# Where the first transposing loads stand in the load queue, and where the first block of x is turned

## The chip, the cores and the metric

The kernel runs on one core of one Trainium2 chip. The metric is the device time of one execution in microseconds (us); a time given for a kernel is the median of its runs. A profile shows one further execution on the same kind of core.

## The reference

Two independent attention blocks, A and B, of the same size (S = 2048 rows, D = 640, 32 heads of 20), whose outputs stand side by side in the result:

```python
B, S, D = 1, 2048, 640            # bf16; wqkv (640, 1920), wo (640, 640)

def _A_ref(x, wqkv, wo):          # causal softmax attention in a window of 256 keys
    H = 32; Dh = D // H; W = 256
    qkv = (x @ wqkv).reshape(B, S, 3, H, Dh).transpose(2, 0, 3, 1, 4)
    q, k, v = qkv[0], qkv[1], qkv[2]
    scores = jnp.einsum("bhqd,bhkd->bhqk", q, k) * (Dh ** -0.5)
    mask = (idx[:, None] - idx[None, :] >= 0) & (idx[:, None] - idx[None, :] < W)
    p = softmax(jnp.where(mask, scores, -1e9))
    o = jnp.einsum("bhqk,bhkd->bhqd", p, v)
    return o.transpose(0, 2, 1, 3).reshape(B, S, D) @ wo

def _B_ref(x, wqkv, wo):          # linear attention over all rows
    ...
    pq, pk = phi(q), phi(k)       # phi(t) = where(t > 0, t + 1, exp(t)) + 1e-6
    kv = jnp.einsum("bhsd,bhse->bhde", pk, v)
    z = jnp.einsum("bhsd->bhd", pk)
    o = jnp.einsum("bhqd,bhde->bhqe", pq, kv) / (jnp.einsum("bhqd,bhd->bhq", pq, z)[..., None] + 1e-6)
    return o.transpose(0, 2, 1, 3).reshape(B, S, D) @ wo

return jnp.concatenate([_A_ref(A_x, A_wqkv, A_wo), _B_ref(B_x, B_wqkv, B_wo)], axis=-1)
```

## The kernel before

The rows are worked on in four blocks of 512 (SB). D is cut into five tiles of 128 (KT), so a projection is a chain of five matmuls that add up in one bank of PSUM; the banks named "dense" are four and are used in turn. An evacuation (`evac`) copies a finished bank to SBUF; it goes to ACT or to DVE after a running count of what each has been given. Every engine works through its instructions in the order in which the program lists them, and waits where an operand isn't there yet. All loads and stores are issued on SP's queue, in program order as well.

A matmul needs x with its columns on the partitions, that is, transposed. There are two ways to that. `load_x` and `load_part` let the DMA transpose while it loads (`dma_start_transpose`, in the profile DMA_TRANSPOSE): a whole block of x at line 162, a quarter of a block at line 938. `load_x_first` does it for the first block of A's x alone: two plain loads bring 256 rows each (line 172, into a tile that the profile calls phi), and `transposes(i)` has PE turn them in blocks of 128 x 128 (line 178, ten for each half), after which DVE copies one 128-row block to xA and ACT the other (lines 184 and 186).

At the start SP issues, in this order: x's first half; v's weights wA in two parts (line 948: kt 0 and 1, 320 KB, then kt 2 to 4, 480 KB; K0 = 2 is the cut); x's second half; the raw weights of q and of k (line 335, 800 KB each, into tiles that the profile calls qpad and kpad); the transposing load of A's second block, xA[1]; B's key weights wB (line 156, 800 KB); the transposing load of B's first block, xB[0].

PE runs 28 dummy products (line 197) while the first load is on its way, then turns x's first half, runs three more dummies, and projects v of the first block. v is made by 128 rows and half of the heads at a time, eight chains of five products of 320 columns (line 412). The first four chains are made by `v_abreast`: the first two products of all four, then the other three of each. Then x's second half is turned, and `v_proj` makes the other four chains one after the other. Among them stand the calls of `regroup`, in which DVE, ACT and POOL rearrange the raw weights of q (behind the sixth chain) and of k (behind the eighth) into wqk, in which the heads are spaced by 32 columns (lines 350, 353 and 356).

Then come three chains of q and two of k (line 277, five products of 512 columns each), and with them the main loop starts: tiles of scores (line 762), their exponentials on ACT (line 780), masks on POOL (line 794), products with v (line 821). Between the tiles, `take` fills PE with the chains of a `plan`, sorted by due times written out by hand: the rest of q and k of the first block, q of the second block (the first use of xA[1]), B's keys (`b_keys(0)`, the first use of xB[0] and wB), and so on to the output projections. The plan holds DMA issues too: `keep_x(0)` (line 927) writes xB[0] to DRAM for later; the writes and reads at lines 375 and 384 move the part of q and k of the first block that belongs to heads of the groups from 5 on to other partitions by way of DRAM.

The order at the start, as the program lists it:

```python
    raw = [load_raw(i) for i in range(2)]
    xA[1] = load_x("A", 1)
    load_w("B", B_wqkv, 1, nc.sync)
    xB[0] = load_x("B", 0)
    ...
    v_abreast(xA[0], v_tok[0], by_tokens[0:4], K0)
    transposes(1)
    a_v0 = v_proj(xA[0], v_tok[0], by_tokens[4:])
    run(banks(a_v0, 2))
    regroup(0, raw[0], dve_copy, in_turn(act_copy, pool_copy))
    run(a_v0)
    regroup(1, raw[1], in_turn(dve_copy, act_copy), in_turn(act_copy, pool_copy))
```

Of the kernel before, what the change touches and what calls it, by code (L numbers as in the profile page):

```python
# [92 lines left out]
def kernel(  # L93
# [10 lines left out]
    nc = tc.nc  # L104
    _, S, D = A_x.shape
    KT = D // P
# [46 lines left out]
    def load_w(n, src, i, eng):  # L153
        wv = src.rearrange("(kt p) n -> p kt n", p=P)
        cols = slice(i * D, (i + 1) * D)
        eng.dma_start(out=w_sb[n][:, :, cols], in_=wv[:, :, cols])

    xsrc = {"A": A_x[0], "B": B_x[0]}

    def load_x(n, s):  # L160
        t = xp.tile([P, KT, SB], BF16, name=f"x{n}")
        nc.sync.dma_start_transpose(out=t[:], in_=xsrc[n][s * SB : (s + 1) * SB, :])
        return t

# [25 lines left out]
    def warm_up(wait):  # L190

        z = op.tile([P, TPS, D], BF16, name="osb")
        nc.vector.memset(z[:, 0, 0:P], 0.0)
        ps = dps.tile([P, SB], F32, name="dense")
        for n in wait:
            for _ in range(n):
                nc.tensor.matmul(
                    ps[:, 0:P], lhsT=z[:, 0, 0:P], rhs=z[:, 0, 0:P], start=True, stop=True
                )
            yield  # L200
# [27 lines left out]
    def flush(before=None):  # L228

        while later and (before is None or later[0][0] <= before):  # L230
            later.pop(0)[1]()
# [9 lines left out]
    def settle(all=True):  # L241
        while posts and (all or posts[0][0] <= begun[0]):
            posts.pop(0)[1]()
# [12 lines left out]
    def evac(dst, src, n=SB, to=None):  # L256

        if to is None:
            to = "A" if load["A"] < load["D"] + AHEAD else "D"
        load[to] += n + COPY  # L260
        if to == "A":
            nc.scalar.activation(out=dst, in_=src, func=ACT.Copy)
        else:
            nc.vector.tensor_copy(out=dst, in_=src)

    def bank(wide=False):
        flush(begun[0] - 2)
        begun[0] += 1
        settle(False)
        if wide:  # L270
            return dps.tile([P, 2 * SB], BF16, name="dense")
        return dps.tile([P, SB], F32, name="dense")
# [32 lines left out]
    def banks(g, n):  # L305

        for _ in range(n):
            for c in g:
                yield c
                if isinstance(c, End):  # L310
                    break

    xA, xB = {}, {}
    q_pad, k_pad, v_tok = {}, {}, {}
# [7 lines left out]
    for c in range(KT):  # L322
        m = EXTRA * c
        while m < EXTRA * (c + 1):
            n = min(EXTRA * (c + 1) - m, DH - m % DH)
# [3 lines left out]
    def load_raw(i):  # L329

        pl, name = ((qp, "qpad"), (kp, "kpad"))[i]
        t = pl.tile([P, NG, SB], BF16, name=name)
        raw = t.rearrange("p g q -> p (g q)")[:, 0 : KT * D].rearrange("p (k n) -> p k n", n=D)
        wv = A_wqkv.rearrange("(kt p) n -> p kt n", p=P)
        nc.sync.dma_start(out=raw, in_=wv[:, :, i * D : (i + 1) * D])
        return raw

    def regroup(i, src, heads, extras):

        def four(g):  # L340
            return src[:, :, 4 * DH * g : 4 * DH * (g + 1)].rearrange("p k (j d) -> p k j d", d=DH)

        for c in range(KT):
            dst = wqk[:, i, :, c * P : (c + 1) * P].rearrange("p k (j e) -> p k j e", e=32)
            heads(dst[:, :, :, 0:DH], four(c))
            for _, row, g, d, n in [piece for piece in pieces if piece[0] == c]:
                extras(dst[:, :, :, row : row + n], four(g)[:, :, :, d : d + n])
# [10 lines left out]
    def in_turn(*fns):  # L358
        n = [0]

        def copy(dst, src):
            n[0] += 1
            fns[n[0] % len(fns)](dst, src)

        return copy
# [43 lines left out]
    by_tokens = [(tb, i) for tb in range(TPS) for i in range(2)]  # L409

    def v_product(ps, xt, tb, i, kt):
        nc.tensor.matmul(  # L412
            ps[:, 0 : hh * DH],
            lhsT=xt[:, kt, tb * P : (tb + 1) * P],
            rhs=w_sb["A"][:, kt, i * hh * DH : (i + 1) * hh * DH],
            start=(kt == 0),
            stop=(kt == KT - 1),
        )

    def v_rows(ps, dst, tb, i):  # L420
        evac(
            dst[:, tb, i * hh : (i + 1) * hh, 0:DH],
            ps[:, 0 : hh * DH].rearrange("p (h d) -> p h d", d=DH),
            hh * DH,
        )

    def v_proj(xt, dst, order):
        for tb, i in order:
            ps = bank()
            for kt in range(KT):  # L430
                v_product(ps, xt, tb, i, kt)
                if kt < KT - 1:
                    yield hh * DH
            v_rows(ps, dst, tb, i)
            yield End(hh * DH)

    def v_abreast(xt, dst, order, k0):
        pss = [bank() for _ in order]
        for ps, (tb, i) in zip(pss, order):
            for kt in range(k0):  # L440
                v_product(ps, xt, tb, i, kt)
        for ps, (tb, i) in zip(pss, order):
            for kt in range(k0, KT):
                v_product(ps, xt, tb, i, kt)
            v_rows(ps, dst, tb, i)

# [470 lines left out]
    def run(gen):  # L919
        for _ in gen:  # L920
            pass
# [22 lines left out]
    K0 = 2  # L944
# [3 lines left out]
        nc.sync.dma_start(out=w_sb["A"][:, k0:k1, :], in_=wv[:, k0:k1, 2 * D : 3 * D])  # L948
    load_half(1)
    raw = [load_raw(i) for i in range(2)]  # L950
    xA[1] = load_x("A", 1)
    load_w("B", B_wqkv, 1, nc.sync)
    xB[0] = load_x("B", 0)
    dummies = warm_up((28, 3))
    next(dummies)
    transposes(0)
    next(dummies)
    v_tok[0] = v_bufs[0]
    v_abreast(xA[0], v_tok[0], by_tokens[0:4], K0)
    transposes(1)  # L960
    a_v0 = v_proj(xA[0], v_tok[0], by_tokens[4:])
    run(banks(a_v0, 2))
    regroup(0, raw[0], dve_copy, in_turn(act_copy, pool_copy))
    run(a_v0)
    regroup(1, raw[1], in_turn(dve_copy, act_copy), in_turn(act_copy, pool_copy))

    def late_load(n, w):

        if w in (0, 2):
            load_w(n, B_wqkv, w, nc.sync)  # L970
        elif n == "A":

            wj = w.rearrange("(g j d) n -> g d j n", j=4, d=DH)
            for g in range(NG):
                lo, hi = g * DH, min((g + 1) * DH, P)
                if lo < P:
                    nc.sync.dma_start(out=wo_sb[n][lo:hi, 0:4, :], in_=wj[g, 0 : hi - lo])
            for j in range(4):
                for g in range(NG):
                    lo, hi = max(g * DH, P), (g + 1) * DH  # L980
                    if hi > P:
                        nc.sync.dma_start(
                            out=wo_sb[n][32 * j + lo - P : 32 * j + hi - P, 4, :],
                            in_=wj[g, lo - g * DH : DH, j],
                        )
        else:
            g = GH * DH
            whole = w[0 : KT * g, :].rearrange("(c p) n -> p c n", p=g)
            nc.sync.dma_start(out=wo_sb[n][0:g, 0:KT, :], in_=whole)
            nc.sync.dma_start(out=wo_sb[n][0 : D - KT * g, KT, :], in_=w[KT * g : D, :])  # L990
# [91 lines left out]
    for i, (s, parts, selects, done) in enumerate(units):  # L1082
# [7 lines left out]
        if ready and ready[0][0] + LAG <= i:  # L1090
# [3 lines left out]
            _, at = ready.popleft()  # L1094
# [10 lines left out]
    while ready:  # L1105
        take(5500)
        _, at = ready.popleft()
# [36 lines left out]
```

## Time and profile before

| | |
|---|---|
| median of 3 runs | 260.53 us (260.48 to 260.59) |
| the profiled execution: its own time | 261.33 us |
| the profiled execution: span from first to last instruction | 259.6 us |
| PE busy | 247.7 us (95%) |
| ACT, DVE, POOL busy | 200.3 (77%), 177.0 (68%), 171.8 us (66%) |
| DMA moved over the span | 36.35 MB, mean 140 GB/s |
| first product of q on PE | 13.93 us |
| first tile of scores on PE | 19.42 us |

Times within a profile count from its first instruction. PE is the matmul engine, PEld its weight loads, DVE, ACT and POOL the other three compute engines, SPq the instructions on SP's queue that issue DMAs. A row of a timeline gives start, duration, engine, line of the program, operation, tiles (written <- read), the count of instructions merged in the row, and in brackets the engine's idle time before it with what ended it.

### The profile page before, as it was taken

Reading aid. Unit: us, or ns where it says so; the run is one execution under the profiler, and the core shown is the slowest. Engines: PE = TensorE matmul, PEld = TensorE weight load, DVE = VectorE, ACT = ScalarE, POOL = GpSimd, SP = SyncE. Lnnn points to the kernel's source line nnn. Section 1 sums busy time; section 2 is a strip of 40 time slices with the busy share of each in tenths; the row PEclk is TensorE's granted clock in tenths of the full one; section 3 lists DMA queues with packets and bytes.
Section 4 is the critical chain, followed back from the end, with each engine's and each line's share of the span. In section 5 each row is a group of like instructions: output and inputs, shape, how many; then the busy total and the mean of one; then the engine's idle time right before and its main releaser. Section 6 shows DMA issues by size and latency. Waiting matters only on the chain.

```text
span 259.6 us, 10761 instructions
## 1 busy us (share of the span) xinstructions
PE 247.7 (95%) x4722; PEld 142.4 (55%) x4769; DVE 177.0 (68%) x308; ACT 200.3 (77%) x260; POOL 171.8 (66%) x211
## 2 busy tenths in 40 slices
PE   8699999999999999999999999999999999999995
PEld 7444445556445745555456555555456554555573
DVE  0245686786745456866655578599889879978662
ACT  3376887899776788988676788888879998988742
POOL 6113777777696766759485796949767594976800
PEclk9999999999999999999999999999999999999999
DMA  6996579699568993502484591622857286975725
GB/s 186 312 231 182 79 198 136 103 279 216 92 95 247 114 257 88 163 3 48 84 132 122 58 190 43 170 43 59 173 89 174 48 188 168 109 136 120 233 47 186
DMA packets 65012, 36.35 MB, mean 140 GB/s; under 512 B 48197, under 2 KB 63941, under 8 KB 64965
## 3 DMA queue, kind: packets, MB, share of 16 engines
q1 hardware_dynamic: 64965, 35.67, 64.6%
q8 instruction: 37, 0.61, 1.0%
q14 instruction: 10, 0.08, 0.1%
HBM read 14.42 MB, written 9.83 MB: 93 GB/s over the span
## 4 chain that ended last, share of the span: by engine, by line
PE 80%; POOL 6%; issue 4%; ACT 3%; DVE 3%; DMA 3%; SPq 0%; ACTq 0%; DVEq 0%
PE dense L277 43%; PE S_ps L762 10%; PE dense L545 9%; PE dense L821 8%; PE dense L412 7%; POOL p L794 4%; DMA wA<-in_A_wqkv_dram 3%; ACT p L780 2%; POOL plow L794 2%; PE dense L652 1%; PE dense L695 1%; DVE phi L294 1%; ACT e L287 1%; PE dense L624 1%; DVE e L291 1%
## 5 line engine op out<-in xcount | busy, mean ns | idle before, releaser
L780 ACT ACTIVATE p<-S_ps 128x2048 bf16<-128x2048 f32 x76 | 142.4, 1873 | 33.9 <-PE S_ps L762 33.1
L794 POOL TENSOR_SCALAR_AFFINE_SELECT p<-p 128x512 bf16<-128x512 bf16 (+1 forms) x152 | 123.3, 822 | 63.8 <-ACT p L780 58.5
L277 PE MATMUL dense<-xA,wqk 128*128 128x512 bf16 x183 | 47.2, 379 | 1.1 <-issue 0.6
L794 POOL TENSOR_SCALAR_AFFINE_SELECT plow<-p 128x1024 bf16<-128x1024 bf16 x32 | 38.8, 1211 | 2.2
L762 PE MATMUL S_ps<-qpad,kpad 20*64 20x64 bf16 (+3 forms) x1728 | 35.2, 213 | 0.4
L762 PEld LDWEIGHTS <-kpad 20*64 20x64 bf16 (+1 forms) x1728 | 17.4, 100 | 30.0 <-issue 25.5
L834 DVE STREAM_TRANSPOSE T<-dense 128x512 f32<-128x512 f32 x32 | 22.8, 712 | 12.6 <-PE dense L821 12.5
L277 PEld LDWEIGHTS <-wqk 128*128 128x128 bf16 x200 | 18.5, 98 | 20.6 <-issue 1.3
L412 PE MATMUL dense<-wA,xA 128*128 128x320 bf16 x160 | 27.7, 300 | 2.1 <-DMA wA<-in_A_wqkv_dram 1.8
L291 DVE TENSOR_SCALAR e<-e 128x512 bf16<-128x512 bf16 x40 | 22.0, 550 | 10.7 <-ACT e L287 10.1
L294 DVE SCALAR_TENSOR_TENSOR phi<-dense,e 128x512 bf16<-128x512 f32 x40 | 27.7, 692 | 1.5
L821 PE MATMUL dense<-p,vA 128*32 128x64 bf16 (+2 forms) x1152 | 27.1, 223 | 0.5 <-POOL p L794 0.5
L277 PE MATMUL dense<-wB,xB 128*128 128x128 bf16 (+1 forms) x156 | 25.4, 297 | 0.8 <-issue 0.6
L287 ACT ACTIVATE e<-dense 128x512 bf16<-128x512 f32 x40 | 23.4, 594 | 2.5 <-PE dense L277 2.2
L277 PE MATMUL dense<-wo,oT 128*128 128x128 bf16 (+2 forms) x154 | 24.3, 296 | 1.0 <-issue 0.6
L545 PE MATMUL dense<-phi,tok 128*128 128x128 bf16 (+1 forms) x154 | 24.3, 296 | 0.7 <-issue 0.3
L277 PE MATMUL dense<-xB,wB 128*128 128x512 bf16 x90 | 24.2, 380 | 0.6 <-issue 0.3
L821 PEld LDWEIGHTS <-vA 128*32 128x32 bf16 x1664 | 22.2, 96 | 3.5 <-issue 1.4
L277 PE MATMUL dense<-wB,xA 128*128 128x512 bf16 (+1 forms) x156 | 23.4, 297 | 0.5 <-issue 0.3
L851 DVE TENSOR_TENSOR N<-T,recA 128x320 bf16<-128x320 f32 (+1 forms) x28 | 18.7, 668 | 3.1 <-DMA oT<-N 2.2
L412 PEld LDWEIGHTS <-xA 128*128 128x128 bf16 x160 | 14.3, 98 | 11.2 <-issue 3.1
L731 DVE TENSOR_TENSOR tok<-tok,rden 128x640 bf16<-128x640 bf16 x16 | 19.8, 1238 | 0.0
(68 smaller groups left out, 237.7 us busy)
## 6 DMA issues: line engine op xcount, KB each, us to landing
out_dram<-osb SPq DMA_DIRECT2D x7, 640.0 KB
x_scr<-xB SPq DMA_DIRECT2D x4, 640.0 KB
tok<-in_B_x_dram SPq DMA_DIRECT2D x4, 640.0 KB
xB<-x_scr SPq DMA_DIRECT2D x4, 640.0 KB
wB<-in_B_wqkv_dram SPq DMA_DIRECT2D x3, 800.0 KB
q_scr<-qpad SPq DMA_DIRECT2D x16, 60.0 KB
k_scr<-kpad SPq DMA_DIRECT2D x16, 60.0 KB
qpad<-q_scr SPq DMA_DIRECT2D x16, 60.0 KB
```

Of the source, the lines that this page charges most:

```text
L277: nc.tensor.matmul(dst, lhsT=lhs(kt), rhs=rhs(kt), start=(kt == 0), stop=(kt == KT - 1))
L287: nc.scalar.activation(out=view(e), in_=src, func=ACT.Exp)
L291: nc.vector.tensor_scalar(out=e[:], in0=e[:], scalar1=1e-6, scalar2=1.0 + 1e-6, op0=ALU.add, op1=ALU.min)
L294: nc.vector.scalar_tensor_tensor(out=dst, in0=src, scalar=0.0, in1=view(e), op0=ALU.max, op1=ALU.add)
L412: nc.tensor.matmul(ps[:, 0 : hh * DH], lhsT=xt[:, kt, tb * P : (tb + 1) * P], rhs=w_sb["A"][:, kt, i * hh * DH : (i + 1) * hh * DH], start ...
L545: nc.tensor.matmul(out, lhsT=lhs(x, pk)[:, tb, :], rhs=rhs(pk, tb), start=(i == 0), stop=(i == len(blocks) - 1),)
L731: nc.vector.tensor_tensor(out=vh, in0=vh, in1=rden_of[s][:, tb, :, :].to_broadcast([P, H, DH]), op=ALU.mult)
L762: nc.tensor.matmul(columns(S_ps[k0:k1], j, col, n, step), lhsT=kt[32 * j : 32 * j + DH, g, ko + k0 : ko + k1], rhs=q_pad[s][32 * j : 32 * ...
L780: nc.scalar.activation(out=p, in_=S_ps[:], func=ACT.Exp, scale=scale)
L794: nc.gpsimd.affine_select(out=dst, in_=src, pattern=[[0, 4], [0, n // HALF], [sgn, HALF]], compare_op=ALU.is_ge, fill=0.0, base=base, chan ...
L821: nc.tensor.matmul(O_ps[32 * j : 32 * (j + 1), q0 : q0 + n], lhsT=v_flat[kb // TPS % 3][:, at + j * HV : at + j * HV + 32], rhs=columns(p, ...
L834: nc.vector.transpose(out=T.rearrange("p b e -> p (b e)"), in_=O_ps[:])
```

## The change

`load_x` gets a flag with which it first sets one column of each of the tile's five parts to zero on DVE; the transposing load writes the same tile, so SP waits for that before it issues it. The transposing loads of xA[1] and xB[0] are listed behind k's regrouping, the first of them with the flag; wB's load keeps its place and so follows the raw weights directly. `v_abreast` is removed: `v_proj` makes all eight chains of v, x's second half is turned behind two of them, and q's weights are regrouped behind six, as before.

```diff
-    def load_x(n, s):
+    def load_x(n, s, wait=False):
         t = xp.tile([P, KT, SB], BF16, name=f"x{n}")
+        if wait:
+            nc.vector.memset(t[:, :, 0:1], 0.0)
         nc.sync.dma_start_transpose(out=t[:], in_=xsrc[n][s * SB : (s + 1) * SB, :])
         return t
...
-    def v_abreast(xt, dst, order, k0):
-        pss = [bank() for _ in order]
-        for ps, (tb, i) in zip(pss, order):
-            for kt in range(k0):
-                v_product(ps, xt, tb, i, kt)
-        for ps, (tb, i) in zip(pss, order):
-            for kt in range(k0, KT):
-                v_product(ps, xt, tb, i, kt)
-            v_rows(ps, dst, tb, i)
...
     load_half(1)
     raw = [load_raw(i) for i in range(2)]
-    xA[1] = load_x("A", 1)
     load_w("B", B_wqkv, 1, nc.sync)
-    xB[0] = load_x("B", 0)
     dummies = warm_up((28, 3))
     next(dummies)
     transposes(0)
     next(dummies)
     v_tok[0] = v_bufs[0]
-    v_abreast(xA[0], v_tok[0], by_tokens[0:4], K0)
+    a_v0 = v_proj(xA[0], v_tok[0], by_tokens)
+    run(banks(a_v0, 2))
     transposes(1)
-    a_v0 = v_proj(xA[0], v_tok[0], by_tokens[4:])
-    run(banks(a_v0, 2))
+    run(banks(a_v0, 4))
     regroup(0, raw[0], dve_copy, in_turn(act_copy, pool_copy))
     run(a_v0)
     regroup(1, raw[1], in_turn(dve_copy, act_copy), in_turn(act_copy, pool_copy))
+
+    xA[1] = load_x("A", 1, wait=True)
+    xB[0] = load_x("B", 0)
```

## The prediction

> **What bounds the kernel now.** I read the page first, then the chain that ended last for the first 20 us, the timelines of PE and SP, and the DMA rows and windows of the same stretch, because everything that the diff moves lies there.
>
> ```profile
> PE 247.7 (95%) x4722; PEld 142.4 (55%) x4769; DVE 177.0 (68%) x308; ACT 200.3 (77%) x260; POOL 171.8 (66%) x211
> PE 80%; POOL 6%; issue 4%; ACT 3%; DVE 3%; DMA 3%; SPq 0%; ACTq 0%; DVEq 0%
> ```
>
> PE is busy for 95% and makes 80% of the chain that ended last. The DMA's 3% is one wait at the front:
>
> ```profile
> 1.82 6.68 DMA wA<-in_A_wqkv_dram
> 8.50 0.04 issue
> 8.54 1.79 PE dense L412 x12
> 10.33 0.29 PE dense L178 x5
> 10.63 0.03 issue
> 10.65 0.50 DVE xA L186
> 11.15 0.05 issue
> 11.20 2.89 PE dense L412 x20
> 14.09 0.21 PE dense L277
> ```
>
> So up to 8.54 us the end hangs on wA's second part (v's weights, kt 2 to 4), then on PE alone, but for one gap in which PE waits for DVE's copy of x's turned third block. From the first product of q (13.93 us) on, PE is fed almost without a break, so a microsecond won or lost before it should reach the end whole. The PE timeline gives the parts:
>
> ```profile
> 5.35 1.40 PE L412 MATMUL dense<-wA,xA 128*128 128x320 bf16 x8
> 8.54 1.79 PE L412 MATMUL dense<-wA,xA 128*128 128x320 bf16 x12 [1.80 <-DMA wA<-in_A_wqkv_dram]
> 10.17 0.72 PE L178 MATMUL dense<-ident,phi 128*128 128x128 bf16 x10
> 11.20 2.89 PE L412 MATMUL dense<-wA,xA 128*128 128x320 bf16 x20 [0.31 <-DVE xA L186]
> 13.93 5.56 PE L277 MATMUL dense<-xA,wqk 128*128 128x512 bf16 x24
> ```
>
> A row's time runs to the modelled end of its last product, so I take start to start: 12 v products in 10.17 - 8.54 = 1.63 us and 20 in 13.93 - 11.20 = 2.73 us, 0.1365 each; a transpose takes 0.29 / 5 = 0.058. From wA's landing to q's first product: 32 x 0.1365 + 10 x 0.058 = 4.95 of 5.39 us, so the gap on DVE's copy is worth 0.44.
>
> **Part 1: v's first chains.** Before, the first two products of four chains (8) run while wA is awaited, and 32 are left. After, v_proj finishes a chain before it opens the next: 2 products run, then PE stands, and 38 are left. That is 6 x 0.1365 = 0.82 us more behind the landing. The turn of x's second half now follows chain 2, so chains 3 and 4 (10 products, 1.37 us) lie behind it: they need only x's first half, and DVE's copy (0.49 us) and ACT's (0.70) run beside them. The 0.44 gap goes, and costs 0.44 again if that cover fails. A limit to check is the four banks: two go to the transposes, so chain 3 needs chain 1's copy and chain 4 chain 2's. ACT does both, 0.44 us each, from about 9.2 and 9.9; PE wants the banks at about 10.2 and 10.9. It fits. The copies of x wait behind them in ACT's queue, needed at 11.55 (DVE's) and 12.9 (ACT's), ready by 10.7 and 11.2. Sum: 38 x 0.1365 + 0.58 = 5.77 against 5.39, +0.38 us.
>
> **Part 2: the transposing loads.** Before, xA's sits on SP's queue right behind k's raw weights:
>
> ```profile
> 3.37 0.60 SPq L335 DMA_DIRECT2D kpad<-in_A_wqkv_dram  x1
> 4.01 10.03 SPq L162 DMA_TRANSPOSE xA<-in_A_x_dram  x1
> 14.09 0.58 SPq L156 DMA_DIRECT2D wB<-in_B_wqkv_dram  x1
> 14.71 5.43 SPq L162 DMA_TRANSPOSE xB<-in_B_x_dram  x1
> ```
>
> After, wB's load goes at about 4.0, and both transposing loads behind a DVE memset that is queued behind k's regrouping. Does the removal let wA or the raw weights land sooner? wA, x's second half and both raw loads are issued ahead of it in both kernels. The DMA rows tell when transposing packets (small ones) moved: for 4 to 8 us the first line, for 14 to 16 us the second.
>
> ```profile
> DMA packets 855, 1.04 MB, mean 260 GB/s; under 512 B 43, under 2 KB 855, under 8 KB 855
> DMA packets 1712, 0.46 MB, mean 231 GB/s; under 512 B 1696, under 2 KB 1711, under 8 KB 1711
> ```
>
> While wA was on its way nearly nothing small moved: the transposing load was queued, not moving. I take its effect on wA's landing as nothing. The Trainium skill (DMA: Bandwidth & Descriptors, "Queues, rings and completion order") says that each DMA engine consumes the descriptors of a ring in order; by that rule what is issued behind wA takes nothing from it, and the sum stays +0.38; these rows agree. Against it stands the rate (windows): 260, 229, 229 and 321 GB/s in the four microseconds from 4, and 387 in the two after. That dip begins just where the transposing load is issued; it is the first rival.
>
> The raw weights landed at 11.73 (POOL's first regrouping copy) and 13.92; with v ending 0.38 later, q's regrouping (DVE 1.21 us, ACT 0.84) and k's (ACT 2.12, then at about 17 us) still end before PE's chains need them (q from 14.3, k from 17.5 on). wB (800 KB, 2.1 us at 387 GB/s behind k's raw weights) lands near 16 us and is read first at 29.54.
>
> **Part 3: the wait.** The memset writes 128 x 5 elements; the shortest DVE memset of the trace is 0.11 us. Behind it on DVE is q's first evacuation, before which DVE had 0.55 us idle: nothing on the path. On SP the two transposing loads, the copy of xB to DRAM (22.15) and q's and k's writes and reads (25.62 on) queue behind it. k's last DVE copy ended at 14.66 and will end near 15.2, so xA's load goes at 15.3. The nearest row, xB's before, took from 14.71 to 22.15 (the copy that waits for it), 7.4 us, with wB's load ahead of it; so xA lands by 22.7. SP holds one for 5.43, so xB's goes at 20.7 and lands by 28.1. xA's first use is the fifth fill chain, near 24.9 before, 25.3 after; xB's 29.54 before, 29.9 after. Covers 2.6 and 1.8 us, so nothing on the path; q's and k's writes start 1 to 2 us later, but their reads serve heads from group 5 on, ten score tiles (some 2.9 us each) behind the first at 19.42.
>
> **Sum.** +0.38 us on the profiled execution (span 259.6, its own time 261.33, against the median of 260.53 of the runs shown), carried to the median: **260.9 us**. For this case alone 260.5 to 261.4: 0.4 down if wA gains a third of the dip's 1.3 us (first rival), 0.44 up if the gap behind DVE's copy stays.
>
> **Rivals.**
>
> *The plain loads land sooner.* If the dip from 4 to 8 us is the transposing load's doing, (387 - 260) + 2 x (387 - 229) + (387 - 321) = 509 KB moved too little, 1.3 us at 387 GB/s: 260.9 - 1.3 = 259.6. If wA came as soon as PE has done its two products (5.35 + 0.27 = 5.62), 2.9 us, giving 258.0. For it: the dip starts with the issue. Against: it ends at 8 us while SP still holds the load, and loads with no transposing issue near them start slowly as well (13 GB/s in the second microsecond, 233 in the third).
>
> *PE slows in the longer pause (the slower side).* The 28 dummies took 3.17 us, 0.113 each, and the first ten transposes 0.122, the second ten 0.058 to 0.072: PE starts at half its later speed, for some 4 us. The page's clock row shows 9 throughout and doesn't show this. Before, a pause of 1.8 us didn't bring the slow speed back (0.136 a product behind it). After, PE pauses from 5.6 to 8.54, 2.9 us, with only 2 products and 3 dummies ahead. No pause that long is in the trace. It decides if PE's patience is between 1.8 and 2.9 us; another 4 us at half speed costs 2.0: 262.9. The Trainium skill (TensorE: Matmul & The Clock Gate, Part 1) gives free-running windows of about 3.4 us, an idle one of which halves the clock; by that rule 2.9 us doesn't fill a window and nothing is lost, and the 1.8 us pause agrees, but no run here shows how much work keeps a window busy.
>
> *The held loads land late.* If each of them takes as long on SP as the first did (10.03 us, under 1.6 MB of raw weights), xB lands near 36 and PE stands about 6 us at b_keys: 267. It decides from 9.2 us between xB's issue and landing, 1.8 above the row. Against: wB's 800 KB are then done.
>
> *It does nothing measurable at the front*, because another wait there is the same in both: only if q's regrouping, not v, sets q's start; its last DVE copy (of five) ended at 13.71, PE began on the first block at 13.93 without a wait.
>
> **How the numbers follow.** Forecast 0.45, loads sooner 0.33, slow PE 0.13, held loads late 0.08, nothing 0.01. A measurement of this kernel tells about 0.2%, 0.52 us, from no change. Faster: 0.33 of the first rival and 0.02 of the forecast's low end. Within: 0.28 of the forecast's middle (260.5 to 261.05) and 0.01. Slower: 0.15 of its upper end, 0.13 and 0.08. Range: down to 258.8, leaving out the deepest third of the first rival (0.11); up to 262.6, leaving out the late loads (0.08).
>
> **What would show it.** Right: v's products as 2, a pause of 2.9 us to about 8.5, 8, ten transposes, 30 with no idle before them, q's first product near 14.3, xA's load held on SP until about 15.3, no PE wait for xA or xB. The first rival: wA's wait ends before 8 us and the windows from 4 to 8 us carry over 300 GB/s. The second: v products 0.27 us apart behind the pause. The third: PE idle at its first product of xA's second tile or of xB, released by a DMA. The prediction is wrong if wA's landing moves by more than 0.5 us.

## The result, and the profile after

| | before | after |
|---|---|---|
| median | 261.26 us (22 runs) | 262.73 us (22 runs) |
| ratio of the runs | 1 | 1.0043, 95% interval 1.0023 to 1.0064 |
| profiled execution: span | 259.6 us | 260.7 us |
| its mean granted clock of PE | 1.000 | 0.992 |
| first product of q on PE | 13.93 us | 14.97 us |

By the means the kernel is slower by 0.43%, 1.1 us. The 22 runs of before include the three whose median was 260.53 us. The ratio leaves out three runs of after (264.31, 264.37 and 266.12 us) that are over 1.5% above its fastest run; the medians include them.

The profile's page points at PE's clock. In its rows of 40 slices, the clock's row has one digit that isn't 9, in the second slice (6.5 to 13 us); before, the row was 9 throughout:

```profile
PE   6799999999999999999999999999999999999995
PEclk9799999999999999999999999999999999999999
```

The chain that ended last, for the first 20 us of after, answers to the one shown of before:

```profile
1.82 6.04 DMA wA<-in_A_wqkv_dram
7.85 0.04 issue
7.89 2.29 PE dense L414 x8
10.18 0.87 PE dense L180 x10
11.05 4.08 PE dense L414 x30
15.13 0.22 PE dense L279
```

The order is as predicted: 8 products behind wA, ten transposes, 30 products, and no wait for DVE's copy any more. wA came at 7.89, not 8.54. But the first 8 products take until 9.98, 0.26 us each, and the transposes 0.09, where 0.1365 and 0.058 were counted. The windows of after (PE busy, then PEld, DVE, ACT, POOL, then PE's granted clock, DMA share, GB/s) say why:

```profile
5.00:6.00 1.00, 0.44 (x2) 0.20 (x3) 0.00 (x0) 0.43 (x1) 0.21 (x1) 1.00 0.85 211
6.00:7.00 1.00, 0.00 (x0) 0.00 (x0) 0.00 (x0) 0.00 (x0) 0.00 (x0) 1.00 0.95 296
7.00:8.00 1.00, 0.10 (x1) 0.10 (x1) 0.00 (x0) 0.00 (x0) 0.00 (x0) 0.65 0.98 353
8.00:9.00 1.00, 1.00 (x5) 0.53 (x5) 0.00 (x0) 0.05 (x1) 0.00 (x0) 0.50 1.02 376
9.00:10.00 1.00, 1.00 (x6) 0.52 (x5) 0.00 (x0) 0.39 (x1) 0.00 (x0) 0.50 1.08 393
10.00:11.00 1.00, 1.00 (x12) 0.99 (x11) 0.24 (x1) 0.44 (x1) 0.00 (x0) 0.64 1.06 367
```

PE ran at half its clock. A mean of 0.65 in the window from 7 us puts the fall at 7.30, one of 0.64 in that from 10 its end at 10.72: 3.42 us. The windows cut at these points show what PE did in the 3.42 us ahead of the fall:

```profile
3.88:7.30 3.42, 1.42 (x19) 1.01 (x17) 0.49 (x1) 0.70 (x1) 1.33 (x1) 1.00 0.94 262
7.30:10.72 3.42, 2.83 (x15) 1.87 (x15) 0.00 (x0) 0.88 (x2) 0.00 (x0) 0.50 1.05 378
```

It was busy for 1.42 of 3.42 us, 42%, and was slowed for the next such stretch. From wA's landing to q's first product PE took 14.97 - 7.89 = 7.08 us, where the same instructions take 5.72 without a fall (below): 1.36 us for the fall.

The held loads, on SP's timeline, are issued behind k's regrouping, as planned, and nothing on PE waits for them:

```profile
4.16 1.32 SPq L156 DMA_DIRECT2D wB<-in_B_wqkv_dram  x1
15.67 2.83 SPq L164 DMA_TRANSPOSE xA<-in_A_x_dram  x1
18.55 3.94 SPq L164 DMA_TRANSPOSE xB<-in_B_x_dram  x1
24.52 0.35 SPq L919 DMA_DIRECT2D x_scr<-xB  x1
```

xB had landed by 24.5 us, 6 us ahead of its first use at 30.58.

### The profile page after: what moved, and what is told of

It is laid out like the page before. It is cut to its first block, busy times and chain, and to the rows that moved or that the text cites. A ratio compares the mean times of both kernels' runs of the same rounds, so it can differ in the third digit from the quotient of the medians.

```text
span 260.7 us, 10762 instructions
## 1 busy us (share of the span) xinstructions
PE 248.3 (95%) x4722; PEld 142.7 (55%) x4769; DVE 177.4 (68%) x309; ACT 200.5 (77%) x260; POOL 171.9 (66%) x211
## 4 chain that ended last, share of the span: by engine, by line
PE 79%; POOL 6%; issue 4%; ACT 4%; DVE 3%; DMA 2%; SPq 0%; ACTq 0%; DVEq 0%
PE dense L279 42%; PE S_ps L754 10%; PE dense L537 9%; PE dense L813 8%; PE dense L414 7%; POOL p L786 4%; ACT p L772 2%; DMA wA<-in_A_wqkv_dram 2%; POOL plow L786 2%; DVE e L293 1%; DVE phi L296 1%; ACT e L289 1%; PE dense L644 1%; PE dense L687 1%; PE dense L616 1%
## 5 line engine op out<-in xcount | busy, mean ns | idle before, releaser
L414 PE MATMUL dense<-wA,xA 128*128 128x320 bf16 x160 | 28.6, 308 | 2.7 <-DMA wA<-in_A_wqkv_dram 2.5
```

Source lines behind the costliest of these rows:

```text
L414: nc.tensor.matmul(ps[:, 0 : hh * DH], lhsT=xt[:, kt, tb * P : (tb + 1) * P], rhs=w_sb["A"][:, kt, i * hh * DH : (i + 1) * hh * DH], start ...
```

## The experiments

Two theories were set against each other first. C: the time is lost to the fall of PE's clock. O: it is lost to the order of v's products. L, a third, blames late loads. A "fall" below is an execution whose mean granted clock is at most 0.994 (the others have 0.998 and more). All kernels ran beside runs of the kernel before on their chip, and the ratios are to those.

| kernel | transposing loads | v products ahead of wA | falls | ratio to before (95%) |
|---|---|---|---|---|
| before | early | 8 | 0 of 98 | 1 |
| after | held | 2 | 17 of 22 | 1.0043 (1.0023 to 1.0064) |
| e1_held_abreast | held | 8 | 1 of 12 | 1.0006 (0.9986 to 1.0026) |
| e2_early_chains | early | 2 | 7 of 12 | 1.0043 (1.0014 to 1.0072) |
| e4_held_two | held | 4 | 4 of 12 | 1.0027 (1.0006 to 1.0048) |
| e6_held_ten | held | 2, 10 more dummies | 3 of 12 | 1.0032 (1.0010 to 1.0053) |
| e3_held_dummies | held | 2, 37 more dummies | 0 of 11 | 1.0031 (1.0011 to 1.0050) |
| e7_early_dummies | early | 2, 37 more dummies | 0 of 12 | 1.0018 (1.0005 to 1.0032) |
| e8_before_dummies | early | 8, 17 more dummies | 0 of 12 | 0.9998 (0.9986 to 1.0011) |
| e5_turned_between | early | 8 | 0 of 12 | 0.9982 (0.9968 to 0.9995) |
| e10_between_held | held | 8 | 0 of 12 | 0.9994 (0.9981 to 1.0007) |

(For before, the 98 are its runs beside the experiments. Of the 19 runs of after that its ratio counts, 14 fell. The ratios are of means; where the text gives medians, it says so.)

**Each part of the change alone.** e1_held_abreast keeps before's order of v and holds the loads:

```diff
-    xA[1] = load_x("A", 1)
     load_w("B", B_wqkv, 1, nc.sync)
-    xB[0] = load_x("B", 0)
...
     v_abreast(xA[0], v_tok[0], by_tokens[0:4], K0)
...
+    xA[1] = load_x("A", 1, wait=True)
+    xB[0] = load_x("B", 0)
```

> The transposing loads held as in the changed kernel, but v's first four chains abreast and x's second half turned behind them, as before: the loads' part of the change alone. Theory C (the changed kernel loses its time to PE's clock, which fell to half for one stretch of 3.4 us behind the pause for wA): the 8 products ahead of wA keep the clock up, so no fall; what is left is wA's landing, 7.85 us in the profile of the changed kernel against 8.50 before. If the held loads brought that, 0.65 us faster than before; if it is only one execution's landing, 0.0. Theory O (the time goes to the order of v's products, six more behind wA): the same values, as the order is the old one. Theory L (the held loads cost the time themselves, by arriving late): 1.1 us slower, as the changed kernel.

It is level with before, 260.80 against 260.85 us by the medians. Its PE timeline is before's, 0.6 us earlier, gap included:

```profile
7.95 1.79 PE L414 MATMUL dense<-wA,xA 128*128 128x320 bf16 x12 [1.30 <-DMA wA<-in_A_wqkv_dram]
9.57 0.72 PE L180 MATMUL dense<-ident,phi 128*128 128x128 bf16 x10
10.60 2.89 PE L414 MATMUL dense<-wA,xA 128*128 128x320 bf16 x20 [0.31 <-DVE xA L188]
```

That 0.6 us is one execution's: the median didn't move. L's loss of 1.1 us (a ratio of 1.0042) and a gain of 0.65 us (0.9975) both lie outside the interval, so L falls, and so does such a gain from holding the loads. One of the 12 executions fell, although PE's order is that of before.

e2_early_chains is the other part alone, the loads early and v by chains (against after):

```diff
     raw = [load_raw(i) for i in range(2)]
+    xA[1] = load_x("A", 1)
     load_w("B", B_wqkv, 1, nc.sync)
+    xB[0] = load_x("B", 0)
...
-    xA[1] = load_x("A", 1, wait=True)
-    xB[0] = load_x("B", 0)
```

> The chains' part of the change alone: the transposing loads early as before, v by v_proj from the first chain on, x's second half turned behind two chains. Theory C: the pause is 5.6 to 8.5 us, the clock falls, and the stretch at half speed costs about 1.3 us beside 0.4 for the order: 1.7 us slower than before, clock below 1.00 from about 7 to 11 us. Theory O: 0.4 us slower, clock 1.00. Theory L: 0.4 slower at the most.

It has the whole loss, 1.0043, and the falls, in 7 of 12 executions. These ran 262.66 to 263.68 us, the other five 259.91 to 261.18. The profiled execution has no fall: wA came at 7.04, and PE's pause was 1.0 us. The five without a fall are 0.26 us faster than before by the means, although their order leaves more work behind wA, which fits an early wA in them. So the fall seems to depend on when wA lands; only one of the 12 is profiled. O alone doesn't make the two groups.

**Fill the pause.** e3_held_dummies is after with 37 more dummies ahead of v:

```diff
-    dummies = warm_up((28, 3))
+    dummies = warm_up((28, 40))
```

> The changed kernel with 40 dummy products of 128 columns instead of 3 ahead of v's first chain (37 more, 2.1 us at 0.056 each), so that PE is busy through most of the pause; the second block of x is copied in that time. Theory C: clock 1.00 throughout, 1.3 us faster than the changed kernel, that is 0.3 us faster than before if wA lands 0.65 sooner, 0.4 slower if it doesn't. Theory O: as slow as the changed kernel (1.1 us slower than before). Theory L: the same 1.1 us slower.

No execution fell, as C said. Its profile gives the order's own price:

```profile
8.55 1.25 PE L414 MATMUL dense<-wA,xA 128*128 128x320 bf16 x8 [0.96 <-DMA wA<-in_A_wqkv_dram]
9.63 0.72 PE L180 MATMUL dense<-ident,phi 128*128 128x128 bf16 x10
10.19 4.24 PE L414 MATMUL dense<-wA,xA 128*128 128x320 bf16 x30
14.27 1.03 PE L279 MATMUL dense<-xA,wqk 128*128 128x512 bf16 x3
```

14.27 - 8.55 = 5.72 us, where before took 5.39: 0.33. But the median is 0.9 us above before, between C's 0.4 and O's 1.1, and the interval (0.3 to 1.3 us) holds both. So the clock decides for C, and the time doesn't: the kernel isn't clearly faster than after, whose interval overlaps. What the falls cost in the mean is therefore not shown by filling the pause.

**How much work keeps the clock.** e4_held_two runs the first products of two chains ahead of wA (against before; the loads are held as in e1_held_abreast):

```diff
-    v_abreast(xA[0], v_tok[0], by_tokens[0:4], K0)
+    v_abreast(xA[0], v_tok[0], by_tokens[0:2], K0)
     transposes(1)
-    a_v0 = v_proj(xA[0], v_tok[0], by_tokens[4:])
-    run(banks(a_v0, 2))
+    a_v0 = v_proj(xA[0], v_tok[0], by_tokens[2:])
+    run(banks(a_v0, 4))
```

> The transposing loads held; the first products of two chains (4 instead of 8 or 2) ahead of wA, then the rest of these two, x's second half, and the other six chains. PE pauses from about 5.9 to 7.9 or 8.5 us. Theory C: it tells where the clock falls: with 2.0 us of pause it may stay, then 36 products and ten transposes follow wA, 5.5 us against 5.4 before, so 0.1 slower than e1_held_abreast; if it falls, 1.3 us slower than that. Theory O: 0.1 us slower than e1_held_abreast, clock 1.00. Theory L: as the changed kernel.

4 of 12 fell: between the 1 of 12 with 8 products and the 17 of 22 with 2. e6_held_ten is after with ten more dummies:

```diff
-    dummies = warm_up((28, 3))
+    dummies = warm_up((28, 13))
```

> The changed kernel with 13 dummies instead of 3 ahead of v's first chain (10 more, 0.56 us). In the changed kernel the stretch of 3.41 us ahead of the fall held 1.41 us of PE work, in the kernel before 1.71 and no fall; with ten dummies more it is near 2.0. Theory C+O, if the busy share of such a stretch decides: falls in few of the executions (at most one in three, against three in four), 0.4 to 0.8 us slower than before. If a pause of a given length decides, about half of the executions fall as with two chains abreast: 1.0 slower.

3 of 12 fell, and the kernel is 0.5 us slower than before by the median. Its profiled execution is one of the three. The clock means of 0.53 (window from 8 us) and 0.76 (from 11) put the stretch at 8.06 to 11.48, 3.42 us again, and the windows cut there are

```profile
4.64:8.06 3.42, 1.41 (x22) 1.17 (x20) 0.49 (x1) 0.70 (x1) 0.57 (x1) 1.00 0.98 324
8.06:11.48 3.42, 3.39 (x19) 2.39 (x19) 0.49 (x1) 0.88 (x2) 0.22 (x1) 0.50 1.06 378
```

PE was busy for 1.41 us ahead of the fall, as in after (1.42), though the ten dummies were to bring it to 2.0: the stretch lies elsewhere, so that some of the work fell ahead of it.

The trace's record of PE's clock tells where the stretches lie. It begins in each of the 13 profiles with a change to full speed: at 3.89 us in after, 4.66 in e6_held_ten, 5.04 in before, and 6.21 at the latest (e4_held_two). What came ahead of that isn't in the record; the rows give 1.00 there, so they don't show the slow start that the prediction noted. Each later change in it, that behind the end of the program included, comes a whole number of stretches of 3.413 us behind the first. So a pause can lie across two stretches in one execution and inside one in another. Before's pause of 1.8 us was nearly all in one:

```profile
5.04:8.45 3.41, 1.71 (x14) 0.90 (x12) 0.25 (x1) 0.70 (x1) 0.17 (x1) 1.00 0.92 276
```

With every profile cut at these points, the clock fell behind 15 stretches (13 of them at the program's end), and in none of these was PE busy for more than 1.41 us; in all others it was busy for at least 1.71. Whether the chip goes by this share or by the idle time right ahead of such a point (1.70 us in before, 1.86 in after) these runs don't tell. Nor do 3 falls of 12 decide it: they fit the expectation by the busy share, but the half that a pause's length would give isn't far off for 12 executions.

In e6_held_ten, q's first product came at 15.44, 7.35 us behind wA's landing at 8.09: this fall cost 1.63 us.

**What is left of e3's loss.** e7_early_dummies is e2_early_chains with 40 dummies, e8_before_dummies is before with 20:

```diff
-    dummies = warm_up((28, 3))
+    dummies = warm_up((28, 40))     # e8_before_dummies: (28, 20)
```

> Transposing loads early, v by v_proj from the first chain on, 40 dummies: e3_held_dummies without the held loads. Open is why that was 0.9 us slower than before without any fall of the clock, where the order of the products should cost 0.4. Theory H (the held loads, or wB's load in their place, let wA land later in that kernel): 0.4 slower than before. Theory D (the order and the dummies themselves cost it): 0.9 slower again.

> The kernel before with 20 dummies instead of 3 (17 more, 0.95 us): they end near 6.3 us, the 8 first products near 7.4, still ahead of most landings of wA (7.2 to 9.0 us by the spans of the runs of before). Theory D for the excess of e3_held_dummies, by way of the dummies: slower than before by about 0.5. Otherwise 0.0 to 0.1 slower.

17 more dummies in before's order cost nothing that shows (e8, 0.3 us at most by its interval); 37 more, as in e3 and e7, were not tried in that order. e7 is 0.56 us slower than before by the medians, between the two expectations. Whether x's second half lands too late for the earlier turn was asked by turning it behind three chains (e9_turn_behind_three), beside e7_early_dummies once more, unchanged (e11_early_dummies_again):

```diff
-    run(banks(a_v0, 2))
+    run(banks(a_v0, 3))
     transposes(1)
-    run(banks(a_v0, 4))
+    run(banks(a_v0, 3))
```

> As e7_early_dummies (transposing loads early, v by v_proj, 40 dummies), but x's second half is turned behind three chains instead of two, 0.68 us later. Open is why the kernels with this order and no fall of the clock were 0.6 and 0.9 us slower than before, where their profiles show 5.72 us from wA's landing to q's first product against 5.39, 0.33 more. If x's second half often lands too late for the turn behind two chains (the profiles show no such wait, but each is one execution), this one is faster than e7_early_dummies, 0.3 slower than before. If not, it is as e7_early_dummies.

> e7_early_dummies once more, unchanged, as the comparison for e9_turn_behind_three on the same chip: 0.3 us slower than before if its profile speaks for its executions, 0.6 if there is more that the profile doesn't show.

1.0029 (1.0011 to 1.0047) and 1.0027 (1.0011 to 1.0043): the two are level, so nothing speaks for a late second half, though a difference of 0.3 us would be within the noise. The profiled execution of e11_early_dummies_again has q's first product at 13.77, 5.71 us behind wA at 8.06, and yet a span of 261.2 us. It lost its time far behind the change, in a pause that nothing in the profile ended:

```profile
90.79 0.23 PE L537 MATMUL dense<-ones,phi 128*128 128x1 bf16 x3 [1.43 <-issue]
```

In the other profiles the span is 245.7 to 246.1 us more than q's first product (before 245.67), here 247.4. Why PE stands there, and whether such pauses make up the 0.3 to 0.6 us by which these kernels exceed the order's 0.33, stays open.

**A version without the gap.** e5_turned_between keeps before's loads and its eight early products, and fills the gap behind the turn with the rest of the fourth chain; the copies of the first four chains go to ACT and DVE in turn:

```diff
-        def transposes(i):
-            for tb in (2 * i, 2 * i + 1):
+        def transposes(*tbs):
+            for tb in tbs:
...
-        for ps, (tb, i) in zip(pss, order):
+        for n, (ps, (tb, i)) in enumerate(zip(pss, order)):
             for kt in range(k0, KT):
                 v_product(ps, xt, tb, i, kt)
-            v_rows(ps, dst, tb, i)
+            v_rows(ps, dst, tb, i, to[n])
+            then.get(n, lambda: None)()
...
-    v_abreast(xA[0], v_tok[0], by_tokens[0:4], K0)
-    transposes(1)
+    v_abreast(
+        xA[0], v_tok[0], by_tokens[0:4], K0, "ADAD",
+        {2: lambda: transposes(2), 3: lambda: transposes(3)},
+    )
```

> The loads as before (transposing loads early), the first products of four chains ahead of wA as before; but the third block of x is turned behind the third chain and the fourth block behind the fourth, and the four chains' evacuations go to ACT, DVE, ACT, DVE, so that DVE's copy of the third block lies beside the rest of the fourth chain and the second turn. Theory C+O (clock falls cost 1.3 us where they occur, products and idle time behind wA cost their own time): no idle time behind wA, q's first product 4.95 us behind wA's landing instead of 5.39, no fall of the clock: 0.4 us faster than before. If the gap before the third block's chains moves on (to ACT's copy of the fourth block, or to the evacuations): 0.0.

```profile
8.13 1.38 PE L412 MATMUL dense<-wA,xA 128*128 128x320 bf16 x9 [1.15 <-DMA wA<-in_A_wqkv_dram]
9.35 0.44 PE L178 MATMUL dense<-ident,phi 128*128 128x128 bf16 x5
9.63 0.57 PE L412 MATMUL dense<-wA,xA 128*128 128x320 bf16 x3
10.04 0.44 PE L178 MATMUL dense<-ident,phi 128*128 128x128 bf16 x5
10.38 2.89 PE L412 MATMUL dense<-wA,xA 128*128 128x320 bf16 x20
13.10 1.67 PE L277 MATMUL dense<-xA,wqk 128*128 128x512 bf16 x6
```

No idle time stands behind the first row; q starts 13.10 - 8.13 = 4.97 us behind wA, as expected (4.95). 0.9982 (0.9968 to 0.9995): 0.47 us faster than before by the means, 0.23 by the medians; the interval ends 0.1 us short of no change.

e10_between_held is the same with the loads held, by the edit of e1_held_abreast:

> e5_turned_between with the transposing loads held as in the changed kernel. If holding them does nothing for wA's landing (e1_held_abreast was level with before): 0.4 us faster than before, level with e5_turned_between (0.47 by the means). If it brings wA sooner in the order that has no idle time behind wA: more than that.

260.68 against 260.74 us by the medians, 0.9994 (0.9981 to 1.0007): holding the loads adds nothing here either. The two intervals overlap, but this one includes no change, although its q starts 4.98 us behind wA as well. So a gain of some 0.4 us is shown by the profiles and by e5's runs, and not by e10's.

## Why the prediction was right or wrong

The direction and the range held. The forecast itself did not: 0.38 us is 0.15%, below the interval's 0.23%, and what came on top is the rival on PE's pause, which had a chance of 0.13. That the range held was luck: the rival's own price, 262.9, lies above its end of 262.6, though the prediction names only the late loads as left out. The result stayed inside because not every execution falls and a fall cost less than reckoned.

- *Part 1, the order of v's products:* right in the profiles. 5.77 us were reckoned from wA's landing to q's first product, 5.72 measured in e3_held_dummies; the gap on DVE's copy went and the banks sufficed. By the means, though, the four kernels with v by chains, 37 more dummies and no fall (e3, e7, e9, e11) lost 0.6 to 0.9 us, more than the profiles account for.
- *Part 2, the loads:* right, as far as the runs can tell: taking the transposing load away from behind the raw weights does not bring wA the 1.3 us of the first rival (1.0006 in e1_held_abreast). In the profiles wA came at 8.54, 7.04, 8.13, 7.80, 8.21, 8.64 and 8.06 us with the load early (mean 8.06), and at 7.89, 7.95, 8.55, 7.78, 8.09 and 8.37 with it held (mean 8.11). The dip of the rate stays without it (252, 211, 296 GB/s in after from 4 to 7 us): the first rival falls. The Trainium skill's rule on the order of a ring, as cited in the prediction (DMA: Bandwidth & Descriptors, "Queues, rings and completion order"), agrees with these landings.
- *wA's landing, taken as one number:* wrong to rely on. By its own signs the prediction would be wrong (wA's landing moved by 0.65 us, more than 0.5) and the first rival half true (the wait ended before 8 us, at 7.89, but the rate didn't stay over 300 GB/s). The profile of before was a late one of a spread of 1.6 us. The 13 landings have a standard deviation of 0.4 us, so no single execution's landing could show the first rival true or false.
- *Part 3, the wait:* right, and with more room: xA's load was issued at 15.67 (15.3 reckoned), xB landed by 24.5 (28.1 at the latest), PE waited for neither.
- *The sum's missing term:* the fall of the clock. The rival had the mechanism (the pause grows, with only 2 products ahead of it), its place and nearly its price: 2.0 us for 4 us at half speed were reckoned, 1.36 and 1.63 were lost in the two profiled falls of 3.42 us. The step that failed is its chance, from the sentence that "2.9 us doesn't fill a window". The pause needn't fill one: in after it was 2.5 us. The Trainium skill (TensorE: Matmul & The Clock Gate, Part 1) has windows of about 3.4 us, and the measured 3.42 us agree; that an idle window is needed for the fall is not what these runs show, as 42% busy didn't prevent it. That 17 of 22 executions fall, not all, goes with where the stretch lies and when wA lands.
- *What the falls explain of the loss:* By the sum for the 19 runs of the ratio, 0.33 + 14/19 x 1.36 to 1.63 us is 1.3 to 1.5 us, 0.51% to 0.59%, inside the interval. With the 0.6 to 0.9 us of the kernels without a fall in place of 0.33 it would be 1.6 to 2.1 us, mostly above the interval's 1.7. So the order of v's products brings the loss and the falls, as e2_early_chains shows, but how the 1.1 us divide between its own price and the falls stays open.

## What to carry to other kernels

A pause of PE of some 2 us can cost more than its length, as the work behind it may run at half speed. Where a change lengthens a wait of PE or moves work from ahead of it to behind it, count how much of 3.4 us around the pause PE is busy (here the clock fell at 1.41 us and less and stayed at 1.71 and more), and keep work there. Products of chains that are still incomplete are a good filler, as they also leave less behind the wait. A landing time read from one profile is one draw: before a cause is built on it, compare it over several runs, or through a kernel that changes that cause alone.

## What the runs showed of the hardware that was not expected

PE's clock fell to half with PE busy for 1.41 and 1.42 of the 3.42 us ahead of it, and both profiled falls lasted 3.42 us. The points at which it can change lay 3.413 us apart and elsewhere in the program in each profile (full speed from 3.89 us in after, from 6.21 in e4_held_two). In before's profile PE was busy for 1.71 us of the stretch that holds its pause; none of before's 98 executions fell. One and the same load order let wA's second part land anywhere from 7.04 to 8.64 us. And a PE pause of 1.43 us that nothing in the profile ended, 77 us behind the edited stage, appeared in one profile of a kernel whose other profile lacks it.
